# A cached-attention block for one decoded token on one Trainium2 core: each pair's keys and values arrive in two loads instead of one

## The chip, the core and the metric

The kernel runs on one core of one Trainium2 chip. The metric is the device time of one execution in microseconds (us); smaller is better. The engines are named as in the profile: PE (TensorE), PEld (its weight loads), DVE (VectorE), ACT (ScalarE), POOL (GpSimd) and SP (SyncE, which here issues nearly all transfers). DMA stands for the core's 16 DMA engines, which copy from HBM into the on-chip memory (SBUF).

## The reference

One new token for each of two sequences passes through a pre-layernorm block: attention over a cache of 8192 keys and values for each of 32 heads, and a dense layer with a squared ReLU. All is float32. Cut to what matters:

```python
# x: [2, 1, 512], k_cache and v_cache: [2, 32, 8192, 128]
def attention(x):
    q = (x @ wq).reshape(B, Sq, H, Dh).transpose(0, 2, 1, 3)
    scores = einsum("bhqd,bhkd->bhqk", q, k_cache) * Dh ** -0.5
    o = einsum("bhqk,bhkd->bhqd", softmax(scores), v_cache)
    return o.transpose(0, 2, 1, 3).reshape(B, Sq, H * Dh) @ wo

h = x + attention(layernorm(x))
r = maximum(layernorm(h) @ w1 + b1, 0)
out = h + (r * r) @ w2 + b2
```

The cache is 512 MiB, 8 MiB for each of the 64 pairs of a head and a sequence, and every byte of it is used once.

## The kernel before, in words

**Staging.** For each pair the host has laid keys and values side by side in a tensor `kvd[pair]` of 128 rows of 64 KiB: in each row the first `HALF` elements (32 KiB) are keys, the last `HALF` are values. On chip there is a `ring` of three slots of the same shape (8 MiB each, one row per partition). `load(tile, src, sem)` issues one transfer on SP's queue and adds 16 to a semaphore when it has landed; slot k has the semaphore `LD[k]`. The weights use the same slots: `wqd` goes to slot 2 at the start, and at the end `wod` goes to slot 1 (in two loads, with rows of 40 KiB and of 24 KiB), and `w1d` (rows of 28.1 KiB) and `w2d` (four loads, with rows of 16, 8, 2 and 2 KiB) go to slot 2.

**SP** issues `wqd` and the pairs 0 and 1, then, in a loop of three pairs per round, waits for `FREE` (given once per pair by DVE) and issues the next pair's load. The last two pairs and the weights follow in the same manner.

**One pair** passes through four engines, and semaphores order them:

1. PE waits for `QUERY` (the pair's query column stands in `qc`) and for `LD[u]`, then for each of two halves c of the 8192 keys runs `front(c, ring[u])`: it waits for a score buffer (`BUFFER`) and issues eight matmuls of 512 columns into the PSUM tile `s[c]`, the last of which gives `SCORES`.
2. DVE runs `maxes(i, c)`: it waits for `SCORES`, takes the row maximum into `nm` and gives `MAXED`. After both halves it copies the next query into `qc` and gives `QUERY`.
3. ACT runs `exps(i, c)`: it waits for `MAXED`, takes the exponential in place with its sum, and gives `EXPED`.
4. DVE then waits for `EXPED` and runs four `product`s per half: each multiplies 1024 values per partition (in place, in the slot) by the exponentials and sums them into `ac`. After both halves it drains and gives `FREE`.

`take(engine, sem, n)` waits for a semaphore and takes n off again. PE and DVE are written through a recorder, so nearly all their instructions carry line 54 in the profile; tiles tell them apart (`s<-slots,qc` is `front`, `nm<-s` is `maxes`, `slots<-slots,s` is `product`).

**The end.** PE and DVE leave their loops after 63 pairs. The last pair (`LAST`, slot 0) is written out by hand, interleaved with the softmax weights of the other 62 pairs of finished heads (`shift`, `weighted`, `sums`, `scaled`, `folded`, `heads`). Then come the projection with `wod` (`projected`), the second layernorm, the dense layer with `w1d` and `w2d`, the copy to `res`, and the store to `out`.

Of the kernel before, what the change touches and what calls it, by code (L numbers as in the profile page):

```python
# [20 lines left out]
LAST = BH - 1  # L21
ROUNDS = LAST // 3
HALF = NC * NQ * CS
# [76 lines left out]
def attention_block_kernel(nc, xd, kvd, wqd, wod, w1d, w2d, out):  # L100
    p = Program(nc)
    pe, dve, act, pool, sp = p.pe, p.dve, nc.scalar, nc.gpsimd, nc.sync
# [5 lines left out]
    ring = [slots[:, k * ROW : (k + 1) * ROW] for k in range(3)]  # L108
# [40 lines left out]
    pm = [nc.alloc_psum_tensor(f"pm{k}", (P, 512), F32).ap() for k in range(2)]  # L149

    LD = [p.sem(f"load{k}") for k in range(3)]
    SM, LO = p.sem("small"), p.sem("wo_b")
    LW1 = p.sem("w1")
    LW2 = [p.sem(f"w2_{k}") for k in range(len(W2_PIECES))]
# [3 lines left out]
    def load(tile, src, sem):  # L158
        sp.dma_start(tile, src).then_inc(sem, 16)  # L159

    W1 = ring[2][:, : DB * F].rearrange("p (d f) -> p d f", f=F)
    b1T = ring[2][:, DB * F : DB * F + FB]
    b2T = ring[2][:, DB * F + FB : W1_ROW]
# [1 line left out]
    WO = ring[1].rearrange("p (h c) -> p h c", c=D)  # L165

    load(ring[2], wqd, LD[2])
    load(ring[0], kvd[0], LD[0])
    load(ring[1], kvd[1], LD[1])
    with sp.Fori(0, ROUNDS - 1) as r:  # L170
        i = r * 3
        for u in range(3):
            t = (2 + u) % 3
            p.take(sp, FREE)
            load(ring[t], kvd[i + (2 + u)], LD[t])
    p.take(sp, FREE)
    load(ring[2], kvd[LAST - 1], LD[2])
    p.take(sp, FREE)
    load(ring[0], kvd[LAST], LD[0])
    p.take(sp, FREE)  # L180
    load(WO[:, :HA], wod[:, :HA], LD[1])
    load(WO[:, HA:], wod[:, HA:], LO)
# [84 lines left out]
    def at(tile, pair, n, off=0, size=None):  # L267
        size = n if size is None else size
        return tile[:, bass.ds(pair * n + off, size)]
# [4 lines left out]
    def front(c, slot):  # L274
        p.take(pe, BUFFER)
        for n in range(CS // 512):
            for j in range(NQ):
                c0 = (c * NQ + j) * CS + n * 512
                ins = pe.matmul(s[c][32 * j : 32 * j + 32, n * 512 : (n + 1) * 512], qc, slot[:, c0 : c0 + 512], start=True, stop=True)
        ins.then_inc(SCORES, 1)  # L280

    def maxes(pair, c):
        p.take(dve, SCORES)
        dve.tensor_reduce(at(nm, pair, NC, c, 1), s[c], axis=AX.X, op=ALU.max, negate=True).then_inc(MAXED, 1)

    def exps(pair, c):
        p.take(act, MAXED)
        act.activation(s[c], s[c], AF.Exp, bias=at(nm, pair, NC, c, 1), scale=1.0,  # L288
                       accum_out=at(ls, pair, NC, c, 1)).then_inc(EXPED, 1)

    def product(pair, c, e, base):
        v = piece(base + (HALF + (c * NH + e) * CS), CS)
        return dve.scalar_tensor_tensor(v, v, 1.0, s[c], op0=ALU.mult, op1=ALU.mult,
                                        accum_out=at(ac, pair, NC * NH, c * NH + e, 1))

    first = pe.cut()
    for u in range(3):
        p.take(pe, QUERY)
        p.take(pe, LD[u], 16)
        for c in range(NC):  # L300
            front(c, ring[u])
    pairs = pe.cut()

    with act.Fori(0, ROUNDS * 3) as i:
# [5 lines left out]
    def body(i, base):  # L310
        for c in range(NC):
            maxes(i, c)
        dve.tensor_copy(qc, qs[:, bass.ds(i + 1, 1)].to_broadcast([P, 32])).then_inc(QUERY, 1)
        for c in range(NC):
            p.take(dve, EXPED)
            for e in range(NH):
                ins = product(i, c, e, base)
            ins.then_inc(BUFFER, 1)
        dve.drain().then_inc(FREE, 1)
        return dve.cut()  # L320

    dve.emit(opening)
    with dve.engine.Fori(0, ROUNDS) as r:
        with dve.engine.Fori(0, 3) as u:
            dve.emit(body(r * 3 + u, u * ROW))
# [35 lines left out]
    def invert(lo, nb, bank, tok):  # L361
        p.after("dve", tok)
        return p.tell("dve", dve.reciprocal(rl[:, lo : lo + nb], bank[:, :nb]))

    def scaled(lo, nb):
        aw4 = aw[:, lo * NC * NH : (lo + nb) * NC * NH].rearrange("p (i c e) -> p i c e", c=NC, e=NH)
        ac4 = ac[:, lo * NC * NH : (lo + nb) * NC * NH].rearrange("p (i c e) -> p i c e", c=NC, e=NH)
        w4 = by_pair(wt, lo, nb)[:, :, :, None].to_broadcast([P, nb, NC, NH])
        tok = p.tell("dve", dve.tensor_tensor(aw4, ac4, w4, op=ALU.mult))
        p.after("dve", tok)  # L370
        as3 = acs[:, lo * NH : (lo + nb) * NH].rearrange("p (i e) -> p i e", e=NH)
        return p.tell("dve", dve.tensor_tensor(as3, aw4[:, :, 0, :], aw4[:, :, 1, :], op=ALU.add))

    def folded(lo, nb, tok):
        p.after("pe", tok)
        as3 = acs[:, lo * NH : (lo + nb) * NH].rearrange("p (i e) -> p i e", e=NH)
        for e in range(NH):
            ins = pe.matmul(pm[0][32 * e : 32 * e + 32, :nb], fold, as3[:, :, e], start=True, stop=True)
        return p.tell("pe", ins)
# [16 lines left out]
    def last_products(c, es):  # L396
        for e in es:
            ins = product(LAST, c, e, 0)
        return ins
# [9 lines left out]
    t_l = sums(0, NG, pm[1], t_w)  # L409
    t_a = scaled(0, NG)  # L410
    front(1, ring[0])
    maxes(LAST, 0)
    exps(LAST, 0)
    t_f = folded(0, NG, t_a)
    t_l = invert(0, NG, pm[1], t_l)
    p.take(dve, EXPED)
    last_products(0, (0, 1))
    maxes(LAST, 1)
# [49 lines left out]
    for d in range(DB):  # L468
        for j in range(NQ):
            ins = pe.matmul(y[32 * j : 32 * j + 32, :], xs[:, d, :], W1[:, d, j * FQ : (j + 1) * FQ],  # L470
                            start=(d == 0), stop=(d == DB - 1))
# [70 lines left out]
```

## Time and profile before

| | before |
|---|---|
| median of 3 runs | 1303.01 us (1302.87 to 1303.05) |
| the profiled execution, its own time | 1302.71 us |
| its span, first to last instruction | 1301.3 us |
| DMA | 561.13 MB, mean 431 GB/s |
| busy, share of the span | PE 31%, PEld 8%, DVE 59%, ACT 12%, POOL 0% |
| mean granted TensorE clock | 0.662 |

The span is that of one profiled execution; its own time is 1.4 us longer than the span and 0.3 us under the median of the runs. In the profile's groups of instructions, the columns are: line, engine, operation, output<-inputs, shape, count, then busy time in all and the mean of one in ns, then the idle time of the engine just before them and what ended most of it. A transfer's "us to landing" counts from the start of its issue on SP to the last of its 16 semaphore increments.

### The profile page before, as it was taken

What the parts mean: (1) busy time and instruction counts of PE and PEld (TensorE: products, weight loads), DVE (VectorE), ACT (ScalarE), POOL (GpSimd) and SP (SyncE); (2) the same over time, 40 slices, a digit from 0 to 9 for tenths busy, and PEclk for the clock granted to TensorE, in tenths of its full rate; (3) what the DMA queues carried; (4) which work ended last, traced back from release to release, by engine and by line L of the source; (5) the groups of instructions that cost most, each with busy time, mean ns of one, the idle gap of its engine ahead of it and who ended that gap; (6) DMA issues with size and microseconds to landing.
All of it is one profiled execution on the core that took longest, in us unless ns stands there. A gap on an engine that the chain in (4) does not pass through costs nothing. (4 is left out here: it accounts for less than half of the span.)

```text
span 1301.3 us, 8752 instructions
## 1 busy us (share of the span) xinstructions
PE 401.4 (31%) x2384; PEld 107.9 (8%) x2384; DVE 761.7 (59%) x1267; ACT 160.3 (12%) x268; POOL 0.7 (0%) x6
## 2 busy tenths in 40 slices
PE   3223223323323313313313322322322331331347
PEld 1000000000000000000000000000000000000013
DVE  1375565575565566566466566557457556556564
ACT  0011011011011011111111101101101101101111
POOL 0000000000000000000000000000000000000000
PEclk9576666566666667666666657666666756666668
DMA  9999999999999999999999999999999999999998
GB/s 419 419 449 421 448 421 449 421 437 433 423 445 423 447 423 447 421 443 427 429 439 423 447 423 447 421 447 423 437 433 423 445 423 447 423 447 421 439 423 368
DMA packets 10520, 561.13 MB, mean 431 GB/s; under 512 B 1170, under 2 KB 1298, under 8 KB 1556
## 3 DMA queue, kind: packets, MB, share of 16 engines
q1 hardware_dynamic: 10512, 561.07, 99.7%
q8 instruction: 3, 0.05, 0.0%
q14 instruction: 1, 0.01, 0.0%
q10 hardware_dynamic: 4, 0.00, 0.0%
HBM read 561.00 MB, written 0.07 MB: 431 GB/s over the span
## 5 line engine op out<-in xcount | busy, mean ns | idle before, releaser
L54 PE MATMUL s<-slots,qc 128*32 128x512 f32 x2048 | 362.6, 872 | 859.4 <-PEq L54 859.4
L54 DVE SCALAR_TENSOR_TENSOR slots<-slots,s 128x1024 f32 (+1 forms) x512 | 589.5, 1217 | 2.3 <-DVEq L54 1.0
L54 DVE TENSOR_REDUCE nm<-s 128x1024 f32 (+1 forms) x128 | 156.8, 1225 | 488.9 <-DVEq L54 488.9
L288 ACT ACTIVATE s<-s,nm 128x1024 f32<-128x1024 f32 x128 | 139.3, 1088 | 1090.9 <-ACTq L97 1090.9
L54 PEld LDWEIGHTS s<-slots,qc 128*32 128x32 f32 x2048 | 91.4, 153 | 1129.5 <-issue 1129.4
L54 DVE DVE_READ_ACCUMULATOR slots<-slots,s (+1 forms) x512 | 42.3, 83 | 0.0
L288 ACT ACTIVATION_READ_ACCUMULATOR s<-s,nm (+1 forms) x128 | 24.7, 193 | 0.0
L54 PE MATMUL s<-slots,xr 128*32 128x512 f32 (+1 forms) x96 | 12.6, 684 | 8.8 <-PEq L54 8.2
L54 DVE COPY qc<-qs 128x32 f32 (+1 forms) x64 | 11.0, 172 | 0.0
L54 DVE STREAM_TRANSPOSE big<-s 128x512 f32<-128x512 f32 x2 | 1.4, 718 | 16.1 <-PE s L54 16.1
L54 PE MATMUL pm<-slots,big 128*32 128x512 f32 x64 | 10.6, 782 | 0.0
L54 PE MATMUL pm<-nq,pick_all 128*128 128x496 f32 (+1 forms) x4 | 2.6, 742 | 17.3 <-DVE nq L54 17.3
L54 DVE COPY xT<-pm 128x8 f32<-128x8 f32 x1 | 0.2, 167 | 9.5 <-PE pm L54 9.5
L54 PE MATMUL pm<-ident,xrow 2*128 2x2 f32 x8 | 1.9, 350 | 10.4 <-DMA xrow<-in_x 10.4
L54 PEld LDWEIGHTS s<-slots,xr 128*32 128x32 f32 x96 | 3.5, 126 | 17.1 <-issue 15.7
L54 PE MATMUL s<-big,pick_all 128*128 128x512 f32 x8 | 4.5, 639 | 0.0
L54 PE MATMUL s<-slots,a 128*2 128x128 f32 x112 | 3.5, 272 | 0.9 <-DMA slots<-in_w2d 0.9
L54 PEld LDWEIGHTS pm<-slots,big 128*32 128x32 f32 x64 | 2.6, 138 | 5.6 <-issue 5.1
L54 PEld LDWEIGHTS s<-slots,a 128*2 128x2 f32 x112 | 2.7, 84 | 2.3 <-DVE a L54 1.5
L54 DVE COPY res<-s 128x128 f32<-128x128 f32 x1 | 0.3, 291 | 4.4 <-PE s L54 4.4
L54 PEld LDWEIGHTS pm<-ident,xrow 2*128 2x128 f32 x8 | 1.8, 322 | 10.4 <-DMA xrow<-in_x 10.4
L54 DVE TENSOR_REDUCE gm<-pm 128x62 f32<-128x496 f32 (+1 forms) x2 | 0.9, 426 | 2.9 <-PE pm L54 2.9
(64 smaller groups left out, 29.4 us busy)
## 6 DMA issues: line engine op xcount, KB each, us to landing
slots<-in_wod SPq DMA_DIRECT2D x1, 5120.0 KB, 33.6
slots<-in_w1d SPq DMA_DIRECT2D x1, 3593.0 KB, 31.1
slots<-in_wod SPq DMA_DIRECT2D x1, 3072.0 KB, 40.6
slots<-in_w2d SPq DMA_DIRECT2D x1, 2048.0 KB, 35.6
slots<-in_kvd SPq DMA_DIRECT2D x64, 41.1
slots<-in_w2d SPq DMA_DIRECT2D x1, 1024.0 KB, 37.6
slots<-in_w2d SPq DMA_DIRECT2D x2, 256.0 KB, 37.7
out<-res SPq DMA_DIRECT2D x1, 64.0 KB, 1.6
```

The costliest lines, as they stand in the source:

```text
L54: ins = getattr(self.engine, op.name)(*op.args, **op.kwargs)
L288: act.activation(s[c], s[c], AF.Exp, bias=at(nm, pair, NC, c, 1), scale=1.0, accum_out=at(ls, pair, NC, c, 1)).then_inc(EXPED, 1)
```

## The change

Each pair's load is issued as two, one for the keys (first 32 KiB of each row, on `LD[t]`) and one for the values (last 32 KiB, on a new semaphore `LDV[t]`). PE waits for the keys before `front`, as it did for the whole pair, and after both `front`s waits for the values and adds one to a new semaphore `VALUES`. DVE takes `VALUES` ahead of its first wait for `EXPED`. The loads of the weights are as they were.

```diff
+    LDV = [p.sem(f"load_v{k}") for k in range(3)]
+    VALUES = p.sem("values")
...
+    def load_pair(t, i):
+        load(ring[t][:, :HALF], kvd[i][:, :HALF], LD[t])
+        load(ring[t][:, HALF:], kvd[i][:, HALF:], LDV[t])
...
     load(ring[2], wqd, LD[2])
-    load(ring[0], kvd[0], LD[0])
-    load(ring[1], kvd[1], LD[1])
+    load_pair(0, 0)
+    load_pair(1, 1)
     with sp.Fori(0, ROUNDS - 1) as r:
         i = r * 3
         for u in range(3):
             t = (2 + u) % 3
             p.take(sp, FREE)
-            load(ring[t], kvd[i + (2 + u)], LD[t])
+            load_pair(t, i + (2 + u))
     p.take(sp, FREE)
-    load(ring[2], kvd[LAST - 1], LD[2])
+    load_pair(2, LAST - 1)
     p.take(sp, FREE)
-    load(ring[0], kvd[LAST], LD[0])
+    load_pair(0, LAST)
...
+    def values(t):
+        p.take(pe, LDV[t], 16)
+        pe.sem_inc(VALUES, 1)
+
     first = pe.cut()
     for u in range(3):
         p.take(pe, QUERY)
         p.take(pe, LD[u], 16)
         for c in range(NC):
             front(c, ring[u])
+        values(u)
...
         dve.tensor_copy(qc, qs[:, bass.ds(i + 1, 1)].to_broadcast([P, 32])).then_inc(QUERY, 1)
+        p.take(dve, VALUES)
         for c in range(NC):
             p.take(dve, EXPED)
...
     front(1, ring[0])
+    values(0)
     maxes(LAST, 0)
     exps(LAST, 0)
     t_f = folded(0, NG, t_a)
     t_l = invert(0, NG, pm[1], t_l)
+    p.take(dve, VALUES)
     p.take(dve, EXPED)
     last_products(0, (0, 1))
```

On SP's queue, the start and the first pair of the loop stand so before (`free` is `FREE`; an `ISA` row without a wait only sets an address):

```order
L159 DMA slots<-in_wqd 128x16384 [waits barrier_Pool_Activation_PE_DVE_SP_release]
L159 DMA slots<-in_kvd 128x16384 x2
L170 UNCONDITIONAL_BRANCH
L159 ISA [waits free]
L159 DMA slots<-in_kvd 128x16384
```

and so after the change, in the same place:

```order
L161 DMA slots<-in_wqd 128x16384 [waits barrier_Pool_Activation_PE_DVE_SP_release]
L161 DMA slots<-in_kvd 128x8192 x4
L176 UNCONDITIONAL_BRANCH
L161 ISA [waits free]
L161 DMA slots<-in_kvd 128x8192
L161 ISA
L161 DMA slots<-in_kvd 128x8192
```

Each load of 16384 elements a row has become two of 8192; the second follows the first with no wait of its own.

On PE, the first pair of the loop and the head of the second stand so before (`load0` is `LD[0]`):

```order
L54 MATMUL s0<-slots,qc 32x512 [waits query,load0,buffer]
L54 MATMUL s0<-slots,qc 32x512 x7
L54 MATMUL s1<-slots,qc 32x512 [waits buffer]
L54 MATMUL s1<-slots,qc 32x512 x7
L54 MATMUL s0<-slots,qc 32x512 [waits query,load1,buffer]
```

and so after (`load_v0` is `LDV[0]`):

```order
L54 MATMUL s0<-slots,qc 32x512 [waits query,load0,buffer]
L54 MATMUL s0<-slots,qc 32x512 x7
L54 MATMUL s1<-slots,qc 32x512 [waits buffer]
L54 MATMUL s1<-slots,qc 32x512 x7
L54 MATMUL s0<-slots,qc 32x512 [waits load_v0,query,load1,buffer]
```

The matmuls are the same and in the same order; the wait for a pair's values stands ahead of the next pair's first matmul.

## The prediction

> **What bounds the kernel now.** I read the page's summary first, then its DMA queue, its groups and its issues.
>
> ```profile
> span 1301.3 us, 8752 instructions
> PE 401.4 (31%) x2384; PEld 107.9 (8%) x2384; DVE 761.7 (59%) x1267; ACT 160.3 (12%) x268; POOL 0.7 (0%) x6
> q1 hardware_dynamic: 10512, 561.07, 99.7%
> q8 instruction: 3, 0.05, 0.0%
> L54 DVE TENSOR_REDUCE nm<-s 128x1024 f32 (+1 forms) x128 | 156.8, 1225 | 488.9 <-DVEq L54 488.9
> L288 ACT ACTIVATE s<-s,nm 128x1024 f32<-128x1024 f32 x128 | 139.3, 1088 | 1090.9 <-ACTq L97 1090.9
> slots<-in_kvd SPq DMA_DIRECT2D x64, 41.1
> slots<-in_w1d SPq DMA_DIRECT2D x1, 3593.0 KB, 31.1
> ```
>
> No engine is busy more than 59% of the span, while SP's queue keeps the 16 DMA engines busy for 99.7% of it. Its packets can be counted from the code: each load has 128 rows and 16 semaphore writes, the kernel has 73 transfers on this queue (wqd, 64 pairs, 2 of wod, 1 of w1d, 4 of w2d, the output), and 73 x 144 = 10512. So each row is one packet, of 64 KiB for the pairs, and each DMA engine moves 8 rows and writes one semaphore per load. The other engines' idle time is large (488.9 us ahead of the maxima on VectorE, 1090.9 ahead of the exponentials): they wait for data. The question is therefore only whether the same bytes take the queue longer or shorter, and whether the queue could run dry.
>
> The steady pace comes from TensorE's timeline, in which each pair's matmuls begin when its load has landed, and from one stage of the windows view:
>
> ```profile
> 178.99 6.35 PE L54 MATMUL s<-slots,qc 128*32 128x512 f32 x32 [13.56 <-PEq L54]
> 1243.26 5.00 PE L54 MATMUL s<-slots,qc 128*32 128x512 f32 x32 [13.22 <-PEq L54]
> 178.00:1243.00 1065.00, 312.80 (x1760) 79.04 (x1760) 643.13 (x1045) 132.50 (x220) 0.00 (x0) 0.65 1.00 433
> ```
>
> Between the two rows lie 55 pairs (1760 matmuls of this stage over 32), so a pair takes (1243.26 - 178.99) / 55 = 19.350 us, with a DMA share of 1.00 at 433 GB/s. How far the queue is ahead: a pair's load lands 41.1 us after its issue (the last but one row of the first fence), of which 19.35 are its own, so about 21.7 us of other loads lie ahead of it when it is issued.
>
> The end, from the chain view's neighbourhood in the timeline:
>
> ```profile
> 1298.92 0.11 PEld L54 LDWEIGHTS s<-slots,a 128*2 128x2 f32 x8 [0.22 <-DMA slots<-in_w2d]
> 1299.39 0.29 DVE L54 COPY res<-s 128x128 f32<-128x128 f32 x1 [4.40 <-PE s L54]
> 1299.70 0.35 SPq L504 DMA_DIRECT2D out<-res  x1
> ```
>
> The last piece of w2d releases the last weight loads at 1298.92, and the rest of the span is 2.4 us. What delays the last landing delays the end by as much.
>
> **The change part by part.**
>
> Not on the path: the work of SP, TensorE and VectorE.
>
> ```profile
> L159 SPq DMA_DIRECT2D slots<-in_kvd x64: 332/333/426, 1.2 to 1221.0; - x64
> SPq L97 <- SPq L97: 1218.4, 65, 31.2
> 62.35 4.95 PE L54 MATMUL s<-slots,qc 128*32 128x512 f32 x32 [13.68 <-PEq L54]
> 68.95 1.22 DVE L54 SCALAR_TENSOR_TENSOR slots<-slots,s 128x1024 f32 x1
> 78.09 0.08 DVE L54 DVE_READ_ACCUMULATOR slots<-slots,s  x1
> 81.71 5.50 PE L54 MATMUL s<-slots,qc 128*32 128x512 f32 x32 [14.42 <-PEq L54]
> ```
>
> SP issues 64 more transfers of 0.333 us each, 21 us in all, out of 1218 us in which it waits for a free slot; without that cover each pair would pay 0.33 us. The second issue reaches the queue 0.33 us after the first, and 21.7 us of loads lie ahead of both. TensorE gets one more wait and one increment per pair. Behind them in its queue stand the next pair's query, its keys and its first matmul; the values land half a pair (9.7 us) after the keys and the next keys 9.7 us after that, while the matmuls of a pair take 4.95 to 6.35 us, so TensorE stands waiting for values some 3 us and is free long before the next keys. VectorE's new wait stands behind both maxima and the query's copy and ahead of the first product, and it is the products that wait in it. Now products begin 6.6 us after the matmuls do and end 9.2 us later (68.95 to 78.17), so a slot is free about 16 us after its pair has landed. Afterwards the matmuls, maxima and most of the exponentials lie in the time in which the values still travel, and the slot is free about 10 us after they land. The queue's lead grows from 21.7 to about 28 us. A lead that was never used up is worth nothing when it grows, so I cost all of this at 0, in both directions. At the end the last pair's products also come earlier, but the end hangs on w2d, which stands last in the queue.
>
> On the path: 128 rows of 64 KiB become 256 of 32 KiB, and 16 semaphore writes become 32, for each of 64 pairs. The bytes are the same. Per DMA engine this is 8 more rows and one more semaphore write per pair, 512 and 64 in all. No 32 KiB row is in this trace; the nearest are the loads of the weights at the end, with rows of 40, 24, 28.1, 16, 8, 2 and 2 KiB.
>
> ```profile
> L159 SPq DMA_DIRECT2D slots<-in_kvd x1: 338/338/338, 1221.0 to 1221.0; - x1
> DMA to landing us min/median/max: 41.3/41.3/41.3
> L159 SPq DMA_DIRECT2D slots<-in_wod x2: 328/376/425, 1240.9 to 1241.3; - x2
> DMA to landing us min/median/max: 33.6/37.1/40.6
> L159 SPq DMA_DIRECT2D slots<-in_w1d x1: 327/327/327, 1259.3 to 1259.3; - x1
> L159 SPq DMA_DIRECT2D slots<-in_w2d x1: 425/425/425, 1259.6 to 1259.6; - x1
> DMA to landing us min/median/max: 35.6/35.6/35.6
> L159 SPq DMA_DIRECT2D slots<-in_w2d x2: 432/432/432, 1260.6 to 1261.1; - x2
> DMA to landing us min/median/max: 37.7/37.7/37.8
> slots<-in_wod SPq DMA_DIRECT2D x1, 5120.0 KB, 33.6
> slots<-in_wod SPq DMA_DIRECT2D x1, 3072.0 KB, 40.6
> slots<-in_w2d SPq DMA_DIRECT2D x1, 2048.0 KB, 35.6
> slots<-in_w2d SPq DMA_DIRECT2D x1, 1024.0 KB, 37.6
> slots<-in_w2d SPq DMA_DIRECT2D x2, 256.0 KB, 37.7
> ```
>
> The tile views give issue and time to landing, for the last pair's load first, then for wod, w1d (its time to landing stands in the first fence), w2d's first load and its last two; the issues' rows give the sizes. The last pair lands at 1221.0 + 41.3 = 1262.3, the first load of w2d at 1259.6 + 35.6 = 1295.2, the last at 1261.1 + 37.8 = 1298.9. The seven loads in between hold 5120 + 3072 + 3593 + 2048 + 1024 + 2 x 256 = 15369 KB, 1.876 times the 8192 KB of a pair: at a pair's pace 36.3 us, and they took 36.6. They have 7 x 8 = 56 rows per engine where 64 KiB rows would have 15, so 41 more rows, with their share of semaphore writes, cost 0.3 us: 7.3 ns each, and 4.9 to 9.8 if a reading is off by 0.1. The first four alone, whose rows are nearest to 32 KiB, hold 13833 KB (32.7 us at a pair's pace) and took 32.9: 0.2 us over 18.5 more rows, about 12 ns each. I take 8 ns, nearer to the first value, whose reading error is spread over twice as many rows. The sum: 512 x 8 ns = 4.1 us, with ends of 512 x 4.9 ns = 2.5 us and 512 x 12 ns = 6.2 us. A gain in this term is excluded by the sum over seven loads: none of its readings gives a shorter time for shorter rows.
>
> The profiled execution's own time of 1302.7 becomes 1306.8; its median is 0.3 higher, which gives 1307.1.
>
> [...]
>
> **The rivals.**
>
> No change that can be measured (this kernel's runs differ by 0.2 us; I count 0.2%, 2.6 us, as the least that a comparison tells). The extra row costs under 5.1 ns, because part of the 0.3 us at the end is a one-off stall (the page lists three fetches of instructions beside the loads) and not the rows' own. For it: the low end of the reading, 4.9 ns. Against it: the first four loads. About 1305.3. [...]
>
> Much slower: each split load costs a gap of its own. The nearest case is wod, 8 MiB with 64 KiB pitch in two loads, which landed at 1241.3 + 40.6 = 1281.9, 19.6 us after the last pair: 0.25 us more than a pair. If that belongs to the split, 64 x 0.25 = 16 us and 1319. Against it: the five loads after wod then take 17.0 us for 7177 KB, where a pair's pace gives 16.95, with 33 more rows and four more boundaries, so boundaries as such cost next to nothing, and wod's excess looks like a one-off. [...]
>
> Faster: rows of 32 KiB move quicker per byte than 64 KiB ones. The load of w1d, with rows of 28.1 KiB, can be read so: issued at 1259.3, landed 31.1 us later at 1290.4, 8.5 us after wod for 3593 KB, where a pair's pace gives 8.49. With 0.1 us of reading error it took 8.4, a load of 4096 KB would take 9.58 and a pair 19.16, and the kernel would gain 64 x 0.19 = 12 us at most, 1291. It decides from the point at which a 32 KiB row takes less than half a 64 KiB one. Against it: every longer sum of short rows came out above a pair's pace.
>
> That the earlier keys help is no case of its own: the end would have to wait for an engine somewhere, and the queue at 99.7% leaves 3.9 us for start, end and all gaps together.
>
> **How the numbers follow.** Slower by 4.1 us (2.7 to 6.4 with the ends): 0.77. No measurable change: 0.14. Much slower: 0.05. Faster: 0.04. The time is 1307.1, that of the likeliest. The range runs from 1304.7, inside the case of no change, to 1309.4, the upper end of the likeliest, and leaves out the much slower and the faster case and a part of the others. Faster by over 0.2% has 0.04, within 0.2% 0.14, slower by over 0.2% the remaining 0.82.
>
> **What the changed profile would show.** In the queue's row 64 x 144 = 9216 more packets, 19728 in all, for the same bytes, still above 99%; pairs 19.41 us apart on TensorE in place of 19.350 (19.39 to 19.45); VectorE's first product beginning within a microsecond or two of the values' landing; SP's waits for a free slot still above 1180 us; the pairs' loads landing about as far behind their issue as the earlier issue makes them, some 40 to 50 us. I am wrong if pairs stay at 19.35 us or come sooner (the row's price is not there), if they move beyond 19.5 us (a boundary costs more than its rows), or if SP's wait shrinks to little and the DMA share falls (the queue ran dry).

## The result, and the profile after

The changed kernel takes 1307.65 us (median of 5 runs, 1307.60 to 1308.01), the kernel before 1302.87 us (5 runs, 1302.77 to 1303.05). The ratio is 1.0037, 95% interval 1.0027 to 1.0048: 4.8 us slower. The forecast was 1307.1, in a range of 1304.7 to 1309.4.

These lines answer to those of before: from the changed kernel's page the span, the busy times, the DMA queue and the groups that wait; from its waits view SP's wait for a free slot; and from the tile view of the pairs' loads their time to landing, over keys and values together.

```profile
span 1306.3 us, 9128 instructions
PE 401.1 (31%) x2384; PEld 107.4 (8%) x2384; DVE 765.8 (59%) x1267; ACT 160.4 (12%) x268; POOL 0.7 (0%) x6
q1 hardware_dynamic: 19728, 561.07, 99.9%
L54 DVE SCALAR_TENSOR_TENSOR slots<-slots,s 128x1024 f32 (+1 forms) x512 | 589.7, 1216 | 181.8 <-DVEq L54 181.8
L54 DVE TENSOR_REDUCE nm<-s 128x1024 f32 (+1 forms) x128 | 156.7, 1224 | 303.9 <-DVEq L54 303.9
L294 ACT ACTIVATE s<-s,nm 128x1024 f32<-128x1024 f32 x128 | 139.3, 1088 | 1087.1 <-ACTq L97 1087.1
SPq L97 <- SPq L97: 1183.9, 65, 30.5
DMA to landing us min/median/max: 31.0/43.9/60.0
```

The queue moved the same 561.07 MB in 19728 packets in place of 10512 and was full for 99.9% of a span that is 5.0 us longer. The engines do as much as before. VectorE's idle time has only moved. Before, 488.9 us of it lay ahead of the maxima and next to nothing ahead of the products, whose row stood so:

```profile
L54 DVE SCALAR_TENSOR_TENSOR slots<-slots,s 128x1024 f32 (+1 forms) x512 | 589.5, 1217 | 2.3 <-DVEq L54 1.0
```

Now 303.9 us lie ahead of the maxima and 181.8 ahead of the products, 485.7 in all. SP still waits for a free slot during 1184 us.

The pace of the pairs, from TensorE's timeline, and the same stage of the windows view as before:

```profile
189.33 4.95 PE L54 MATMUL s<-slots,qc 128*32 128x512 f32 x32 [13.31 <-PEq L54]
1238.60 5.96 PE L54 MATMUL s<-slots,qc 128*32 128x512 f32 x32 [14.00 <-PEq L54]
178.00:1243.00 1065.00, 313.07 (x1752) 79.05 (x1756) 644.51 (x1043) 131.10 (x218) 0.00 (x0) 0.63 1.00 432
```

Fifty-four pairs lie between the rows: (1238.60 - 189.33) / 54 = 19.431 us per pair, 81 ns more than 19.350, at 432 GB/s in place of 433 and the same DMA share of 1.00. Over 64 pairs 81 ns are 5.2 us, which covers the whole difference (4.8 us between the medians, 5.0 between the spans). The end is as it was:

```profile
1303.94 0.11 PEld L54 LDWEIGHTS s<-slots,a 128*2 128x2 f32 x8 [0.21 <-DMA slots<-in_w2d]
1304.41 0.29 DVE L54 COPY res<-s 128x128 f32<-128x128 f32 x1 [4.38 <-PE s L54]
1304.73 0.34 SPq L518 DMA_DIRECT2D out<-res  x1
```

The last weights are released at 1303.94 by the last piece of w2d, and 2.4 us remain, as before.

### The profile page after: what moved, and what is told of

Its sections match the earlier page's. It is cut to its first block, busy times and chain, and to the rows that moved or that the text cites. A ratio compares the mean times of both kernels' runs of the same rounds, so it can differ in the third digit from the quotient of the medians.

```text
span 1306.3 us, 9128 instructions
## 1 busy us (share of the span) xinstructions
PE 401.1 (31%) x2384; PEld 107.4 (8%) x2384; DVE 765.8 (59%) x1267; ACT 160.4 (12%) x268; POOL 0.7 (0%) x6
## 3 DMA queue, kind: packets, MB, share of 16 engines
q1 hardware_dynamic: 19728, 561.07, 99.9%
## 5 line engine op out<-in xcount | busy, mean ns | idle before, releaser
L54 DVE SCALAR_TENSOR_TENSOR slots<-slots,s 128x1024 f32 (+1 forms) x512 | 589.7, 1216 | 181.8 <-DVEq L54 181.8
L54 DVE TENSOR_REDUCE nm<-s 128x1024 f32 (+1 forms) x128 | 156.7, 1224 | 303.9 <-DVEq L54 303.9
L54 PE MATMUL pm<-nq,pick_all 128*128 128x496 f32 (+1 forms) x4 | 2.6, 742 | 19.3 <-DVE nq L54 19.3
## 6 DMA issues: line engine op xcount, KB each, us to landing
slots<-in_kvd SPq DMA_DIRECT2D x128, 4096.0 KB, 43.9
slots<-in_wod SPq DMA_DIRECT2D x1, 3072.0 KB, 47.8
slots<-in_w2d SPq DMA_DIRECT2D x2, 256.0 KB, 43.9
```

Of the source, the lines that this page charges most:

```text
L54: ins = getattr(self.engine, op.name)(*op.args, **op.kwargs)
```

## The experiments

Three theories could each make 81 ns per pair. R: each extra row costs its DMA engine a constant time, 8 rows per engine and pair (the trace's records of single packets put a 64 KiB row of the kernel before at 2.42 us, and 8 x 2.42 = 19.4 us, about a pair's pace of 19.350). B: the extra load costs it, with its boundary and semaphore writes. W: the new waits and the token (the count in `VALUES` that TensorE gives and VectorE takes) cost it. The diffs are cut and stand against the kernel before, where nothing else is said. Each run's time stands beside runs of the kernel before on the same chip. The pace of the pairs is worked out as above; the two rows of TensorE's timeline are shown for each run on which the verdict rests, 54 pairs apart.

### One load per pair, with rows of 32 KiB

```diff
+    def load_pair(t, i):
+        load(ring[t].rearrange("p (n c) -> p n c", n=2), kvd[i].rearrange("n p c -> p n c"), LD[t])
...
-        "kvd": np.concatenate([k, v], axis=2),
+        "kvd": np.concatenate([k, v], axis=2).reshape(BH, P, 2, ROW // 2).transpose(0, 2, 1, 3),
```

> One load per pair as before, but keys and values stand in HBM as two blocks of 128 rows, so that the load has 256 rows of 32 KiB; waits as before. Theory R (the time goes to the extra rows, about 9 ns each on their DMA engine): 8 more rows per engine and pair, pairs 19.42 us apart, 1307.3 us. Theory B (the time goes to the extra load, its boundary and semaphore writes): 1302.9, pairs at 19.35. Theory W (it goes to the new waits of TensorE and VectorE): 1302.9.

Measured: 1307.73 us (1307.38 to 1307.86), before 1302.73; ratio 1.0038 (1.0025 to 1.0052).

```profile
q1 hardware_dynamic: 18704, 561.07, 99.8%
198.98 6.22 PE L54 MATMUL s<-slots,qc 128*32 128x512 f32 x32 [13.72 <-PEq L54]
1248.10 5.62 PE L54 MATMUL s<-slots,qc 128*32 128x512 f32 x32 [14.34 <-PEq L54]
```

The pairs are 19.428 us apart. The packets are the changed kernel's less 64 x 16 = 1024 semaphore writes. Neither an extra load nor a new wait is in this kernel, and the whole loss is: R.

### Two loads per pair, waited for at once

Against the changed kernel (VectorE's `p.take(dve, VALUES)` goes too, and the last pair is changed in the same way):

```diff
-        load(ring[t][:, HALF:], kvd[i][:, HALF:], LDV[t])
+        load(ring[t][:, HALF:], kvd[i][:, HALF:], LD[t])
...
-        p.take(pe, LD[u], 16)
+        p.take(pe, LD[u], 32)
         for c in range(NC):
             front(c, ring[u])
-        values(u)
```

> The changed kernel's two loads per pair, both on the slot's one semaphore; TensorE waits for 32 ahead of the first matmul, no wait for values and no token. R and B: as the changed kernel, 1307.6 us, pairs at 19.43. W: as before, 1302.9. If the earlier start on the keys had given something back in the changed kernel, this one would be slower than it, over 1308.

Measured: 1307.88 us (1307.74 to 1308.02), before 1302.73; ratio 1.0040 (1.0026 to 1.0054).

```profile
199.18 6.09 PE L54 MATMUL s<-slots,qc 128*32 128x512 f32 x32 [13.87 <-PEq L54]
1248.31 5.47 PE L54 MATMUL s<-slots,qc 128*32 128x512 f32 x32 [14.49 <-PEq L54]
```

19.428 us per pair, as with one load of as many rows: the boundary between two loads and their 16 semaphore writes have no price that these rows show. Against the kernel before it loses 5.15 us, and the changed kernel, whose start on the keys is earlier, 4.8: a difference well inside both intervals, while the pace of the pairs agrees within 3 ns. So no gain from the earlier start is shown.

### The token alone

```diff
         for c in range(NC):
             front(c, ring[u])
+        pe.sem_inc(VALUES, 1)
...
+        p.take(dve, VALUES)
         for c in range(NC):
             p.take(dve, EXPED)
```

> The kernel before with its single loads; TensorE adds one to the new semaphore after each pair's matmuls and VectorE takes it ahead of its first wait for the exponentials. R and B: 1302.9 us, pairs at 19.35. W: up to 1307.6.

Measured: 1302.68 us (1302.44 to 1302.99), before 1302.73; ratio 1.000 (0.9991 to 1.0009).

```profile
198.47 5.09 PE L54 MATMUL s<-slots,qc 128*32 128x512 f32 x32 [13.15 <-PEq L54]
1243.42 6.56 PE L54 MATMUL s<-slots,qc 128*32 128x512 f32 x32 [13.38 <-PEq L54]
```

The pairs are 19.351 us apart. W falls for the token. The wait for the values is not in this run; the two runs above have the loss without it.

### Two loads per pair, of 64 rows each

```diff
+        load(ring[t][:64], kvd[i][:64], LD[t])
+        load(ring[t][64:], kvd[i][64:], LD[t])
```

> Two loads per pair, each of 64 rows of 64 KiB (upper and lower partitions), both on one semaphore, waits as before: rows as before, twice the loads and semaphore writes. R: 64 more semaphore writes per engine at 9 ns or less, 1303.5 us at most. B: 1307.6. Either may be covered by a third effect: if the 16 DMA engines don't share 64 partitions as they share 128, pairs would come far slower, and the run would tell nothing of R and B.

Measured: 2658.26 us, ratio 2.0403 (2.0371 to 2.0434). The pairs came far slower (40.6 us apart), as the expectation has it for a third effect, and the run tells nothing of R and B. The windows view of this run, in the same stage:

```profile
178.00:1243.00 1065.00, 151.87 (x844) 38.12 (x848) 304.02 (x494) 62.68 (x104) 0.00 (x0) 0.56 1.00 208
```

The DMA engines are busy all the time (share 1.00) and move 208 GB/s in place of 433.

### Rows of 16 KiB: in four loads, in one load

```diff
+    def load_pair(t, i):
+        load(ring[t][:, 0 * ROW // 4 : 1 * ROW // 4], kvd[i][:, 0 * ROW // 4 : 1 * ROW // 4], LD[t])
...
-        p.take(pe, LD[u], 16)
+        p.take(pe, LD[u], 64)
```

> Four loads per pair with rows of 16 KiB, on one semaphore, waits as before. R (about 9 ns per extra row): 24 more rows and 3 more semaphore writes per engine and pair, three times the changed kernel's cost, 78 x 3 = 234 ns per pair, 1303 + 15 = 1318 us. B (the boundary): also 3 x 78 ns, 1318. If the cost were a one-off of the step from 64 KiB to anything less: 1307.6.

The other is the kernel with one load of 32 KiB rows, its 2 blocks per pair made 4.

> One load per pair, in HBM four blocks of 128 rows of 16 KiB, so 512 rows per load; waits as before. R: 24 more rows per engine and pair at about 9 ns, 1303 + 14 = 1317 us. B: 1302.9.

Measured: four loads 1317.84 us (1317.67 to 1318.22), ratio 1.0116 (1.0099 to 1.0133); one load 1317.50 us (1317.22 to 1317.61), ratio 1.0112 (1.0095 to 1.0129); before 1302.86. Two rows of the four loads' timeline, then two of the one load's:

```profile
200.38 6.24 PE L54 MATMUL s<-slots,qc 128*32 128x512 f32 x32 [13.80 <-PEq L54]
1257.55 5.02 PE L54 MATMUL s<-slots,qc 128*32 128x512 f32 x32 [13.31 <-PEq L54]
```

```profile
200.60 5.23 PE L54 MATMUL s<-slots,qc 128*32 128x512 f32 x32 [13.11 <-PEq L54]
1257.78 5.70 PE L54 MATMUL s<-slots,qc 128*32 128x512 f32 x32 [14.32 <-PEq L54]
```

Both are at 19.577 us per pair, 227 ns over 19.350, for 24 more rows: 9.5 ns each. Three more loads per pair, or none, make no difference that these rows show. B falls.

### Rows of 8 KiB, in one load

The same kernel with 8 blocks per pair.

> One load per pair, in HBM eight blocks of 128 rows of 8 KiB, 1024 rows per load; waits as before. R, with the 9.5 ns per extra row that the runs with 16 KiB rows showed: 56 more rows per engine and pair, 0.53 us per pair, pairs at 19.88, 1303 + 34 = 1337 us. If the cost per row falls with its length: under 1330.

Measured: 1336.56 us (1336.53 to 1336.60), ratio 1.0259 (1.0244 to 1.0275), before 1302.73.

```profile
203.14 6.23 PE L54 MATMUL s<-slots,qc 128*32 128x512 f32 x32 [13.95 <-PEq L54]
1276.63 5.39 PE L54 MATMUL s<-slots,qc 128*32 128x512 f32 x32 [14.79 <-PEq L54]
```

19.879 us per pair, 529 ns for 56 more rows: 9.4 ns each, down to rows of an eighth of the length.

### Two loads cut at 60 KiB

```diff
+    CUT = ROW - 1024
...
+        load(ring[t][:, :CUT], kvd[i][:, :CUT], LD[t])
+        load(ring[t][:, CUT:], kvd[i][:, CUT:], LD[t])
```

> Two loads per pair, cut at 60 KiB of each row in place of 32 KiB, both on one semaphore, waits as before: as many rows and loads as in the changed kernel, 8 rows of 60 and 8 of 4 KiB per engine and pair. R (a constant time per row): 1307.6 us, pairs at 19.43. If the cost lay in the length of the longest row (32 KiB rows being less efficient per byte): about 1303.3, since 60 KiB rows are nearly as long as 64. If short rows cost more than their constant: over 1308.

Measured: 1307.99 us (1307.84 to 1308.28), ratio 1.0040 (1.0024 to 1.0055), before 1302.73.

```profile
199.41 4.99 PE L54 MATMUL s<-slots,qc 128*32 128x512 f32 x32 [13.27 <-PEq L54]
1248.58 6.05 PE L54 MATMUL s<-slots,qc 128*32 128x512 f32 x32 [13.90 <-PEq L54]
```

19.429 us per pair, the pace of the rows cut in half. The time comes near the 1308 above which short rows would have cost more, but the pace shows nothing of it. Where the rows are cut made no difference here, only how many there are.

### A later release of the slots

The prediction priced the earlier release of the slots at nothing. This tests it from the other side.

```diff
+        for k in range(4):
+            dve.tensor_reduce(extra[:, k : k + 1], big, axis=AX.X, op=ALU.max)
         dve.tensor_copy(qc, qs[:, bass.ds(i + 1, 1)].to_broadcast([P, 32])).then_inc(QUERY, 1)
```

> The kernel before with four more maxima of 1024 columns per pair on VectorE, ahead of the next query's copy (they feed nothing): each slot is released about 4.8 us later, nearly as much as the changed kernel releases it earlier. If a slot's release has no price while the queue has loads ahead: 1302.9 us, pairs at 19.35. If the queue's lead were used up now and then: above 1304, and then the earlier release in the changed kernel would have hidden a part of its cost.

Measured: 1305.40 us (1304.57 to 1306.00), ratio 1.0019 (1.0010 to 1.0029), before 1302.86. Neither 1302.9 nor a loss in the loop. The added work of one pair on VectorE's timeline, two rows of TensorE's in the loop, and TensorE's rows at the end:

```profile
1250.38 4.59 DVE L54 TENSOR_REDUCE extra<-big 128x1 f32<-128x1024 f32 x4
```

```profile
198.50 5.73 PE L54 MATMUL s<-slots,qc 128*32 128x512 f32 x32 [14.18 <-PEq L54]
1243.46 5.49 PE L54 MATMUL s<-slots,qc 128*32 128x512 f32 x32 [14.42 <-PEq L54]
...
1294.33 3.21 PE L54 MATMUL s<-slots,xr 128*32 128x448 f32 x32
1297.47 1.13 PE L54 MATMUL s<-big,pick_all 128*128 128x512 f32 x2
1298.98 1.93 PE L54 MATMUL s<-slots,a 128*2 128x128 f32 x64 [0.38 <-DVE a L54]
1300.72 0.40 PE L54 MATMUL s<-ident,hb 128*2 128x128 f32 x8
1300.94 1.49 PE L54 MATMUL s<-slots,a 128*2 128x128 f32 x48
```

The same rows at the end of the kernel before:

```profile
1290.40 3.21 PE L54 MATMUL s<-slots,xr 128*32 128x448 f32 x32 [0.63 <-DMA slots<-in_w1d]
...
1295.33 1.93 PE L54 MATMUL s<-slots,a 128*2 128x128 f32 x64 [0.66 <-DMA slots<-in_w2d]
...
1297.72 1.60 PE L54 MATMUL s<-slots,a 128*2 128x128 f32 x48 [0.24 <-DMA slots<-in_w2d]
```

The pairs are still 19.351 us apart, so the loop pays nothing. But the end begins with the last loop pair's products, and there the engines were less than 1 us ahead of the transfers: TensorE waited 0.63 us for w1d, 0.66 and 0.24 for w2d. The 4.59 us of added maxima use this up (TensorE starts on w1d 3.9 us later, 1294.33 against 1290.40), and no row of the weights' matmuls waits for a transfer any more. The transfers themselves are not late:

```profile
L160 SPq DMA_DIRECT2D slots<-in_w2d x4: 424/428/432, 1264.7 to 1266.1; - x4
DMA to landing us min/median/max: 30.8/32.8/33.0
```

The last piece of w2d lands at 1266.1 + 33.0 = 1299.1, against 1298.9 before. The run that follows keeps the added work out of the last pairs.

```diff
-    with dve.engine.Fori(0, ROUNDS) as r:
+    with dve.engine.Fori(0, ROUNDS - 1) as r:
         with dve.engine.Fori(0, 3) as u:
-            dve.emit(body(r * 3 + u, u * ROW))
+            dve.emit(body(r * 3 + u, u * ROW, 4))
+    with dve.engine.Fori(0, 3) as u:
+        dve.emit(body((ROUNDS - 1) * 3 + u, u * ROW, 0))
```

> As the later release (four more maxima per pair on VectorE, which feed nothing), but in the first 60 pairs alone; the last four run as before. In the later release pairs stayed 19.35 us apart and the end was late, its engines no longer waiting for the last weights. Theory E (the price of the later release lies in the end alone): 1302.9 us. Theory L (a part of it is paid in the loop, where the queue's lead shrinks): 1304 or more.

Measured: 1302.80 us (1302.30 to 1303.07), ratio 1.000 (0.9991 to 1.0009), before 1302.73. Two rows of TensorE's in the loop, and the pairs' issues:

```profile
198.49 5.83 PE L54 MATMUL s<-slots,qc 128*32 128x512 f32 x32 [14.08 <-PEq L54]
1243.42 5.61 PE L54 MATMUL s<-slots,qc 128*32 128x512 f32 x32 [14.30 <-PEq L54]
slots<-in_kvd SPq DMA_DIRECT2D x64, 36.5
```

The pairs are 19.351 us apart, and a load lands 36.5 us after its issue in place of 41.1. Theory E holds: in the loop a slot can come free 4.6 us later at no price.

## Why the prediction was right

**What bounds the kernel.** Right: the queue is full before and after, and the loss per pair (81 ns), 64 times, is the loss of the kernel. The packets came out as counted, 19728.

**The row's price.** Right in kind, low in size, and as near as it came partly by luck. The prediction took 8 ns per extra row with its share of semaphore writes, 4.1 us. The changed kernel paid 81 / 8 = 10 ns, and the experiments 9.4 to 9.9 ns, so the term was 4.8 to 5.2 us. The reading from the end's seven loads (7.3 ns, within 4.9 to 9.8) had been given more weight than that from the first four (12 ns); the value lies about in the middle of the two. But the end's loads don't hold a price as exactly as that. The same loads, unchanged, stand so in the changed kernel (wod, then w2d):

```profile
L161 SPq DMA_DIRECT2D slots<-in_wod x2: 328/376/425, 1238.7 to 1239.0; - x2
DMA to landing us min/median/max: 40.9/44.4/47.8
L161 SPq DMA_DIRECT2D slots<-in_w2d x4: 424/428/432, 1258.5 to 1259.9; - x4
DMA to landing us min/median/max: 41.8/43.8/44.0
```

The last pair's values landed at 1219.6 + 47.9 = 1267.5 (their row stands further below) and the last piece of w2d at 1259.9 + 44.0 = 1303.9. The seven loads took 36.4 us, 0.1 over the 36.3 that a pair's pace before gives, where the kernel before took 36.6. Read in the same way, their 41 extra rows would have cost 2.4 ns each. Why the weights' rows show less than the pairs' rows paid, no run tells.

The share of the semaphore writes is nothing that can be seen: one load and two with the same rows have the same pace, 19.428 us per pair.

**What was costed at nothing.** Right. The token alone: 1302.68 against 1302.73. The second issue on SP: its waits fell from 1218 to 1184 us, with the queue still full. The earlier release: the queue's lead grew as forecast (the last pair's keys land 38.5 us after their issue, about 9.7 of them their own, which leaves 28.8 against some 28), and it bought nothing that can be told: the two loads waited for at once lack it, and their loss is the changed kernel's within 0.4 us. A later release costs nothing in the loop.

**The rivals.** No measurable change fell with the row's price; it needed less than 5.1 ns. A gap per split load, read from wod's 0.25 us, fell with the pairs of one and of several loads. Wod's excess was a one-off, as the prediction had suspected: in the changed kernel wod, still in two loads, landed at 1239.0 + 47.8 = 1286.8, 19.3 us after the last pair, no more than a pair's pace. In the kernel before, the trace's records of single packets show one of wod's 128 rows of 40 KiB taking 1.98 us where the others took 1.51 to 1.53; it began just as a 16 KiB fetch of instructions ended (1.1 us, at 1271.0). That the fetch caused it is argued from the times alone. So a stall did stand in the reading at the end, as the rival of no change had it, and the row's price was there all the same. Quicker short rows fell: every cut cost time, and the more rows the more.

**What the profile was to show.** Pairs 19.41 us apart, within 19.39 to 19.45: 19.431. SP's waits above 1180: 1184. The pairs' loads 40 to 50 us from issue to landing: 43.9 in the median of keys and values, though single loads reach from 31.0 to 60.0, and the last pair's keys took 38.5 and its values 47.9. The products soon after the values' landing: the last pair's value load and VectorE's first product on it,

```profile
L161 SPq DMA_DIRECT2D slots<-in_kvd x2: 328/378/427, 1219.2 to 1219.6; - x2
DMA to landing us min/median/max: 38.5/43.2/47.9
1267.96 1.22 DVE L54 SCALAR_TENSOR_TENSOR slots<-slots,s 128x1024 f32<-128x1024 f32 x1 [1.77 <-DVEq L54]
```

1219.6 + 47.9 = 1267.5, and the product begins 0.5 us later.

## What to carry to other kernels

Where a full transfer queue sets the time, count the rows that each DMA engine moves: on top of the bytes each extra row of the pairs' loads cost about 9.5 ns here, so 64 KiB rows cut in half lost 0.4%, and cut into 8 KiB 2.6% of the time, while the number of loads and semaphore writes for the same rows cost nothing that these runs can tell. An earlier start on a part of a transfer gained nothing here that the runs can tell (4.8 us lost with it, 5.15 without), because the end waits for the queue and not for an engine; look in the profile at who waits for whom at the end before splitting a load. And a delay that is free in a loop can cost time in the code behind it: the later release was free for 60 pairs and cost 2.5 us through the last ones.

## What the runs showed of the hardware that had not been expected

The time of an extra row was nearly the same for rows of 60 and 4 KiB, 32, 16 and 8 KiB (9.9, 9.75, 9.5 and 9.4 ns), for contiguous blocks as for parts of 64 KiB rows. Which part of a row's transfer takes this time, no run here shows.

Two loads of 64 partitions each, issued one after the other, moved 208 GB/s where one of 128 partitions moves 433, with the DMA engines busy all the time (share 1.00); the kernel took 2.04 times as long, 2658.26 us. What makes them so slow is not shown here: a split by other sets of partitions was not tried.
